# Layer 2 beyond its first 512 tokens: blocks of 256, both products by one level of Strassen's method

## The chip, the cores and the metric

One NeuronCore of a Trainium2 chip runs the whole program. The metric is device time in microseconds (us) of one execution, lower is better. TensorE multiplies matrices, VectorE (DVE in the profile) and ScalarE (ACT) do elementwise work, GpSimd (POOL) is nearly unused, and SyncE (SP) issues the DMA transfers.

## The reference

Attention with a compressive memory over 4 batches, 8 heads, 576 tokens and a head width of 64 gives an activation x of 2304 tokens by 512. Two dense layers follow, each 512 to 2048 to 512:

```python
h = x @ w_in                       # layer 1: 2304x512 by 512x2048
g = np.maximum(h, 0) + np.log1p(np.exp(-np.abs(h)))
x = g @ w_out                      # 2304x2048 by 2048x512
h = x @ w_in2                      # layer 2, the same sizes
r = np.maximum(h, 0)
return (r * r) @ w_out2
```

## The kernel before

Every 32-bit operand of a matrix product is kept as a sum of two 16-bit tensors, a high part and a low part, and each product is three matmuls (high by high, high by low, low by high) that accumulate in one PSUM bank. Attention and layer 1 (L506 to L668) are interleaved and come first. The change touches only layer 2, from L698 to L853, whose weights are W3 (512 by 2048) and W4 (2048 by 512).

Layer 2 handles the first 512 tokens plainly: `plain_h` (L715) makes the hidden activation with matmuls of 512 moving columns, in four rounds of four products of 12 matmuls, while DVE and ACT still split the pieces of W4 (`split_piece`, L404). Then `row_tile` (L817) makes the output, 128 tokens at a time: 48 matmuls whose stationary operand is a 128x128 piece of the activation and whose moving operand is 512 columns of W4.

The other 1792 tokens go in three blocks of 512 and one of 256. For them the first product is already done by one level of Strassen's method (in Winograd's form): `seven_h` (L786) makes seven products of half-size blocks in place of eight, for a pair of 128-row pieces of the hidden width at a time, four pairs to a block, 12 matmuls to a product, 336 to a block. They have 256 moving columns in the blocks of 512 tokens and 128 in the last block. The sums of weight blocks that this needs (`sums_w`, L736, into WS, four calls) and the sums of activation blocks (`x_parts`, L758, into XT) are made by DVE and ACT beside earlier matmuls. DVE adds the seven products up out of PSUM (L805 to L814), and `finish` (L708) applies the activation and splits the result into gg. The second product stays plain: `row_tile` again, 14 tiles for these tokens.

The program is written in this order, and a scheduler of the framework puts each engine's instructions in an order of its own: what comes earlier in the text goes first when it is ready, and where it isn't, later work fills in. All matmul results of this part rotate over eight PSUM banks (pool mm2, L699). Each engine works its own queue in order.

Of the kernel before, what the change touches and what calls it, by code (L numbers as in the profile page):

```python
# [17 lines left out]
P = 128  # L18
# [28 lines left out]
def kernel(  # L47
# [647 lines left out]
    w1_cm.__exit__(None, None, None)  # L695


    bp = ctx.enter_context(tc.tile_pool(name="bp", bufs=2, side="right", reuse_waits="tile"))  # L698
    mm2 = ctx.enter_context(tc.tile_pool(name="mm2", bufs=8, space=PSUM, reuse_waits="tile"))  # L699
    u2 = S_R / S_X2  # L700
    HF = NFC // 2
    gg = {}

    def new_g(j):
        gg[j] = [bp.tile([P, 2, 2, 512], F16, name=f"gg{t}_{j}", bufs=1) for t in range(2)]
        return gg[j]

    def finish(r, hi, lo):  # L708
        act.activation(r, r, AF.Relu, scale=u2)
        act.activation(r, r, AF.Square)  # L710
        act.activation(hi, r, AF.Copy)
        dve.tensor_tensor(lo, r, hi, ALU.subtract)


    def plain_h(j):  # L715
        x = x_t[0]
        new_g(j)
        for h in range(2):
            for i in range(2):
                f = h * HF + j + i  # L720
                ps = mm2.tile([P, 512], F32, tag="mm2", name="h2ps")
                for c in range(NCC):
                    wh, wl = (w[:, c, f * P:(f + 1) * P] for w in W3)
                    xh, xl = (x[:, t * NCC + c] for t in range(2))
                    pe.matmul(ps, wh, xh, start=(c == 0), stop=False)
                    pe.matmul(ps, wh, xl, start=False, stop=False)
                    pe.matmul(ps, wl, xh, start=False, stop=(c == NCC - 1))
                r = bp.tile([P, 2, 512], F32, name="r2", bufs=4)[:, 0]
                act.activation(r, ps, AF.Relu, scale=u2)
                act.activation(r, r, AF.Square)  # L730
                hi, lo = (g[:, h, :, i * 256:(i + 1) * 256] for g in gg[j])
                r = r.rearrange("p (a t) -> p a t", a=2)
                dve.tensor_copy(hi, r)
                dve.tensor_tensor(lo, r, hi, ALU.subtract)

    def sums_w(k, c0):  # L736
        c1 = slice(c0, c0 + 512)
        c2 = slice(DFF // 2 + c0, DFF // 2 + c0 + 512)
        (h11, l11), (h21, l21), (h12, l12), (h22, l22) = [
            [w[:, k + d, c] for w in W3] for d, c in ((0, c1), (0, c2), (2, c1), (2, c2))  # L740
        ]
        T = sp2.tile([P, 4, 512], F32, name="T", bufs=1)
        s1, s2, s3, s4 = (T[:, i] for i in range(4))
        dve.tensor_tensor(s1, h21, h22, ALU.add)
        dve.tensor_tensor(s3, h11, h21, ALU.subtract)
        dve.tensor_tensor(s1, s1, l21, ALU.add)
        dve.tensor_tensor(s3, s3, l21, ALU.subtract)
        dve.tensor_tensor(s1, s1, l22, ALU.add)
        dve.tensor_tensor(s3, s3, l11, ALU.add)
        dve.tensor_tensor(s2, s1, h11, ALU.subtract)  # L750
        dve.tensor_tensor(s2, s2, l11, ALU.subtract)
        dve.tensor_tensor(s4, h12, s2, ALU.subtract)
        dve.tensor_tensor(s4, s4, l12, ALU.add)
        hi, lo = (w[:, :, k, c1] for w in WS)
        act.activation(hi, T, AF.Copy)
        dve.tensor_tensor(lo, T, hi, ALU.subtract)

    def x_parts(t0):  # L758
        n = min(512, NT - t0)
        if n == 512:  # L760
            q = [[x2_at(t0 // NB + t)[:, 4 * d:4 * d + 4] for t in range(2)] for d in range(2)]
            a = 4
        else:
            q = [[x2_at(t0 // NB)[:, 4 * d + t:4 * d + 4:2] for t in range(2)] for d in range(2)]
            a = 2
        (b11, b12), (b21, b22) = q
        T = sp2.tile([P, 4, 512], F32, name="T", bufs=1)
        t1, t2, t3, t4 = (T[:, i, :n].rearrange("p (a t) -> p a t", a=a) for i in range(4))
        dve.tensor_tensor(t1, b12, b11, ALU.subtract)
        dve.tensor_tensor(t3, b22, b12, ALU.subtract)  # L770
        dve.tensor_tensor(t2, b22, t1, ALU.subtract)
        dve.tensor_tensor(t4, b21, t2, ALU.subtract)
        for i, y in enumerate((b11, b21, b22)):
            hi, lo = (z[:, i, :n].rearrange("p (a t) -> p a t", a=a) for z in XT)
# [11 lines left out]
    def seven_h(j, n):  # L786
        hn = n // 2

        def prod(w, x):
            ps = mm2.tile([P, 512], F32, tag="mm2", name="h2ps")[:, :n]  # L790
            for i in range(2):
                o = ps[:, i * hn:(i + 1) * hn]
                for k in range(2):
                    wh, wl = w3_at(w, k, j + i)
                    xh, xl = (y[:, x, k * hn:(k + 1) * hn] for y in XT)
# [3 lines left out]
            return ps  # L799

        r = [bp.tile([P, 2, 512], F32, name="r2", bufs=4) for _ in range(2)]
        (r11, r12), (r21, r22) = [[y[:, i, :n] for i in range(2)] for y in r]
        new_g(j)
        act.activation(r11, prod(0, 0), AF.Copy)
        dve.tensor_tensor(r12, prod(4, 4), r11, ALU.add)  # L805
        dve.tensor_tensor(r22, prod(5, 5), r12, ALU.add)
        dve.tensor_tensor(r21, prod(2, 6), r22, ALU.add)
        p5 = prod(3, 3)
        dve.tensor_tensor(r22, p5, r22, ALU.add)
        dve.tensor_tensor(r12, p5, r12, ALU.add)  # L810
        for h in (1, 0):
            if h == 0:
                dve.tensor_tensor(r11, prod(1, 1), r11, ALU.add)
                dve.tensor_tensor(r12, prod(6, 2), r12, ALU.add)  # L814
            finish(*(z[:, :, :n] for z in (r[h], gg[j][0][:, h], gg[j][1][:, h])))
# [67 lines left out]
```

## Time and profile before

| | us |
|---|---|
| median of 3 runs (lowest, highest) | 972.23 (971.37, 975.96) |
| the profiled execution | 977.67 |
| span of its trace, first to last instruction | 975.7 |
| TensorE busy in the span | 891.3 (91%) |
| DVE busy in the span | 657.2 (67%) |
| ACT busy in the span | 593.9 (61%) |

The trace is of one execution, 5.4 us above the median of the runs. Its span starts at 0, and the stages of layer 2 are read from about 614 us on. A busy time is the union of an engine's instructions; successive matmuls and successive DVE instructions overlap a little in the records, so the step from start to start is shorter than a duration.

### The profile page before, as it was taken

To read this page: it belongs to the slowest core of one execution; us is meant where nothing else is said; L and a number is where in the kernel's file an instruction comes from. 1 tells how busy PE (TensorE), PEld (TensorE's weight loads), DVE (VectorE), ACT (ScalarE), POOL (GpSimd) and SP (SyncE) were. 2 spreads that over 40 slices of the span, in tenths; PEclk is the share of its full clock that TensorE was granted. 3 is DMA by queue.
4 is the path that set the end of the run, shared out by engine and by line. 5 is a ranking of instruction groups with operands and counts; after the bars stand their busy time and mean duration, and the time that the engine had idled before them with its cause. 6 is when DMAs were issued, how large, how long until landed. Compare 5 with 4: busy or idle time off the path is not lost.

```text
span 975.7 us, 21743 instructions
## 1 busy us (share of the span) xinstructions
PE 891.3 (91%) x9012; PEld 682.7 (70%) x9012; DVE 657.2 (67%) x1349; ACT 593.9 (61%) x1110; POOL 2.2 (0%) x10
## 2 busy tenths in 40 slices
PE   4436899899999999999999999999999999999998
PEld 3325688788878788898887888544684585486483
DVE  7998989767747676576846499998894075066050
ACT  7865778678758786787937556562274065056051
POOL 0000000000000000000000000000000000000000
PEclk9999899899999999999999999999999999999999
DMA  9999977676669996767554475620000000000000
GB/s 233 218 244 208 230 152 162 111 116 94 108 105 168 175 152 98 109 117 131 92 87 80 60 238 173 209 65 23 22 1 12 33 1 4 29 12 1 33 13 22
DMA packets 283219, 101.05 MB, mean 104 GB/s; under 512 B 248048, under 2 KB 280816, under 8 KB 283120
## 3 DMA queue, kind: packets, MB, share of 16 engines
q1 hardware_dynamic: 282880, 99.65, 51.6%
q8 instruction: 70, 1.15, 0.5%
q14 instruction: 29, 0.24, 0.1%
q10 hardware_dynamic: 240, 0.02, 0.0%
HBM read 48.78 MB, written 4.72 MB: 55 GB/s over the span
## 4 chain that ended last, share of the span: by engine, by line
PE 56%; DMA 17%; DVE 12%; ACT 8%; issue 4%; SPq 2%; DVEq 0%; ACTq 0%
DMA PT<-p 9%; PE ops L825 6%; PE ops L824 6%; PE ops L826 6%; PE h2ps L797 4%; PE h2ps L798 4%; PE h2ps L796 4%; DMA rawv<-in_v_dram 3%; DMA rawq<-in_q_dram 3%; PE hps L431 2%; PE hps L432 2%; PE s_ps L307 2%; PE hps L433 2%; PE pvt L352 2%; DMA rawk<-in_k_dram 2%
## 5 line engine op out<-in xcount | busy, mean ns | idle before, releaser
L431 PE MATMUL hps<-x,W 128*128 128x256 f16 x576 | 158.7, 277 | 4.4 <-DVE cc L273 3.7
L432 PE MATMUL hps<-x,W 128*128 128x256 f16 x576 | 159.6, 278 | 0.1
L433 PE MATMUL hps<-x,W 128*128 128x256 f16 x576 | 159.3, 277 | 0.0
L449 PE MATMUL xps<-g,W 128*128 128x256 f16 x512 | 139.0, 273 | 1.6 <-DVE g L442 1.5
L448 PE MATMUL xps<-g,W 128*128 128x256 f16 x512 | 137.9, 274 | 2.3 <-ACT g L441 1.4
L450 PE MATMUL xps<-g,W 128*128 128x256 f16 x512 | 139.0, 273 | 0.0
L316 ACT ACTIVATE Pt<-Pt,cs 128x128 f32<-128x128 f32 (+4 forms) x144 | 84.1, 585 | 55.3 <-DVE cs L312 54.8
L307 PE MATMUL s_ps<-KT,qT 128*128 128x128 f16 (+2 forms) x992 | 83.0, 226 | 30.9 <-DVE cs L312 30.2
L825 PE MATMUL ops<-W,gg 128*128 128x512 bf16 x288 | 109.2, 379 | 0.0
L824 PE MATMUL ops<-W,gg 128*128 128x512 f16 x288 | 109.2, 379 | 0.0
L826 PE MATMUL ops<-W,gg 128*128 128x512 f16 x288 | 108.5, 379 | 0.0
L329 DVE TENSOR_TENSOR p<-Pt,p 128x512 f16<-128x512 f32 (+2 forms) x104 | 69.1, 665 | 34.3 <-ACT p L328 34.1
L307 PEld LDWEIGHTS <-qT 128*128 128x128 f16 (+1 forms) x992 | 58.6, 106 | 42.4 <-issue 37.3
L828 ACT ACTIVATE osb<-ops 128x512 f32<-128x512 f32 x18 | 10.7, 597 | 123.6 <-PE ops L826 123.6
L805 DVE TENSOR_TENSOR r<-h2ps,r 128x512 f32<-128x512 f32 (+1 forms) x16 | 9.9, 622 | 108.1 <-PE h2ps L798 107.3
L312 DVE CUSTOM_DVE_ANT_0 Pt<-s_ps,mask 128x128 f32<-128x128 f32 (+3 forms) x128 | 61.8, 483 | 27.7 <-PE s_ps L307 27.3
L352 PE MATMUL pvt<-V,PT 128*128 128x64 f16 (+1 forms) x1392 | 60.7, 198 | 18.8 <-DMA PT<-p 17.0
L352 PEld LDWEIGHTS <-PT 128*128 128x128 f16 (+1 forms) x1392 | 50.7, 104 | 28.0 <-DMA PT<-p 24.5
L328 ACT ACTIVATE p<-Pt 128x512 f16<-128x512 f32 (+2 forms) x104 | 63.0, 606 | 10.2 <-DMA PT<-p 8.9
L432 PEld LDWEIGHTS <-W 128*128 128x128 f16 x576 | 57.3, 99 | 11.8 <-issue 4.7
L798 PE MATMUL h2ps<-XT,WS 128*128 128x256 f16 (+1 forms) x256 | 63.7, 259 | 0.0
L797 PE MATMUL h2ps<-XT,WS 128*128 128x256 f16 (+1 forms) x256 | 63.7, 259 | 0.0
(157 smaller groups left out, 2072.0 us busy)
## 6 DMA issues: line engine op xcount, KB each, us to landing
wst<-in_moe_w_in_dram SPq DMA_DIRECT2D x32, 512.0 KB, 4.7
wst<-in_moe_w_out_dram SPq DMA_DIRECT2D x32, 512.0 KB, 4.5
rawk<-in_k_dram SPq DMA_DIRECT2D x16, 256.0 KB, 4.5
rawq<-in_q_dram SPq DMA_DIRECT2D x16, 256.0 KB, 4.6
rawv<-in_v_dram SPq DMA_DIRECT2D x16, 256.0 KB, 4.5
out_dram<-osb SPq DMA_DIRECT2D x16, 256.0 KB, 2.0
PT<-p SPq DMA_TRANSPOSE x100, 3.4
mraw<-in_M_prev_dram SPq DMA_DIRECT2D x8, 128.0 KB, 4.1
```

The costliest lines, as they stand in the source:

```text
L307: pe.matmul(o[x * n:(x + 1) * n], qT[g][:, t * H + h, x * n:(x + 1) * n], KT[kb][:, h, a - j * P:e - j * P], start=(t == 0), stop=(t == 1),)
L352: pe.matmul(o[r], t[:, o0 + i + y, r], V[kb][:, z, h, :], start=(i == 0 and y + z == 0), stop=(i == nb - 1 and y > 0),)
L431: pe.matmul(o, wh, x[:, c], start=(c == 0), stop=False)
L432: pe.matmul(o, wh, x[:, NCC + c], start=False, stop=False)
L433: pe.matmul(o, wl, x[:, c], start=False, stop=(c == NCC - 1))
L448: pe.matmul(ps, wh, gh, start=(f == f0), stop=False)
L449: pe.matmul(ps, wh, gl, start=False, stop=False)
L450: pe.matmul(ps, wl, gh, start=False, stop=(f == f1 - 1))
L797: pe.matmul(o, wh, xl, start=False, stop=False)
L824: pe.matmul(ps, gh, W4[0][:, f, :], start=(a == 0), stop=False)
L825: pe.matmul(ps, gh, W4[1][:, f, :], start=False, stop=False)
L826: pe.matmul(ps, gl, W4[0][:, f, :], start=False, stop=(a == NFC - 1))
```

## The change

From token 512 on, layer 2 works in seven blocks of 256 tokens (numbers 2 to 8 of nine). `seven_h` has two calls per block, each for four 128-row pieces of one half of the hidden width's halves, seven products of 24 matmuls with 128 moving columns each. The second product, too, takes Strassen's form for blocks 3 to 7: `seven_o` has seven products of 24 matmuls with 256 moving columns, four in its first call and three in its second, and adds them up in o. Blocks 2 and 8 keep a plain second product (`plain_o`, 96 matmuls of 512 columns).

New elementwise work comes with it: `sums_w4` (four calls, into WT) makes the sums of W4's blocks, and `parts` makes, for each half of a block, the sums of activation blocks (GS) beside the activation blocks themselves (GA), each split into high and low. The sums of W3's blocks (`sums`, called by `sums_w3`) take eight DVE additions in place of ten and split the result in two halves. The additions out of PSUM in `seven_h` are as many for each 512 columns as before.

Buffers are laid out anew. One tile TS of 4 x 512 per partition takes the place of T: weight sums use all of it, `x_parts` its first half and the output blocks o its second. The intermediate r of the first half-call lies in a quarter of W3 that is no longer read (RB), XT has a second copy in the room of the first 512 tokens' x, GA has three buffers and GS two. In the plain part for the first 512 tokens, r2 has three buffers of half the size in place of four, and osb one in place of three.

The order of the text per block kb is: `x_parts` of the next block, first half of `seven_h`, first call of `seven_o` for block kb-1, `parts` of the first half, second half of `seven_h`, second call of `seven_o` for kb-1, `parts` of the second half. Two calls of `sums_w4` stand after the four row tiles of the first 512 tokens, one after block 2, one inside block 3.

```diff
+NPL = 1
+W4A = (0, 2)
+W4B = {1: (4,), 2: (6,)}
...
-    bp = ctx.enter_context(tc.tile_pool(name="bp", bufs=2, side="right", reuse_waits="tile"))
+    bp_cm = tc.tile_pool(name="bp", bufs=1, side="right", reuse_waits="tile")
+    bp = bp_cm.__enter__()
...
-                r = bp.tile([P, 2, 512], F32, name="r2", bufs=4)[:, 0]
+                r = bp.tile([P, 512], F32, name="r2", bufs=3)
...
+    def sums(quarters, first, out):
+        T = TS
+        for i, (h, l) in enumerate(quarters):
+            dve.tensor_tensor(T[:, i].rearrange("p (a c) -> p a c", a=h.shape[1]), h, l, ALU.add)
+        a, b, c, d = (T[:, i] for i in range(4))
+        if first:
+            dve.tensor_tensor(d, b, d, ALU.add)
+            dve.tensor_tensor(b, a, b, ALU.subtract)
+            dve.tensor_tensor(a, d, a, ALU.subtract)
+            dve.tensor_tensor(c, c, a, ALU.subtract)
         else:
+            dve.tensor_tensor(a, b, a, ALU.subtract)
+            dve.tensor_tensor(b, d, b, ALU.subtract)
+            dve.tensor_tensor(d, d, a, ALU.subtract)
+            dve.tensor_tensor(c, c, d, ALU.subtract)
+        T = T.rearrange("p q (a c) -> p q a c", a=quarters[0][0].shape[1])
+        for i in (slice(0, 2), slice(2, 4)):
+            act.activation(out[0][:, i], T[:, i], AF.Copy)
+            dve.tensor_tensor(out[1][:, i], T[:, i], out[0][:, i], ALU.subtract)
+    def sums_w3(k, c0):
+        q = [[w[:, k + d:k + d + 1, f * DFF // 2 + c0:f * DFF // 2 + c0 + 512] for w in W3]
+             for d, f in ((0, 0), (0, 1), (2, 0), (2, 1))]
+        sums(q, True, [w[:, :, k:k + 1, c0:c0 + 512] for w in WS])
+    def sums_w4(j):
+        q = [[w[:, d * HF + j:d * HF + j + 2, m * 256:m * 256 + 256] for w in W4]
+             for d, m in ((0, 0), (0, 1), (1, 0), (1, 1))]
+        sums(q, False, [w[:, :, j:j + 2] for w in WT])
+    def x_parts(kb):
+        q = [[x2_at(kb)[:, 4 * d + t:4 * d + 4:2] for t in range(2)] for d in range(2)]
...
+        X = XT[kb % 2]
+        T = TS[:, :, :NB]
...
+    def w4_at(w, j):
+        if w < 3:
+            o, m = ((0, 0), (HF, 0), (HF, 256))[w]
+            return [y[:, o + j, m:m + 256] for y in W4]
+        return [y[:, w - 3, j] for y in WT]
+    GA, GS = {}, {}
+    def seven_h(kb, q):
+        X = XT[kb % 2]
         def prod(w, x):
+            ps = mm2.tile([P, 512], F32, tag="mm2", name="h2ps")
+            for i in range(4):
+                o = ps[:, i * P:(i + 1) * P]
                 for k in range(2):
+                    wh, wl = w3_at(w, k, 4 * q + i)
+                    xh, xl = (y[:, x, k * P:(k + 1) * P] for y in X)
                     pe.matmul(o, wh, xh, start=(k == 0), stop=False)
                     pe.matmul(o, wh, xl, start=False, stop=False)
                     pe.matmul(o, wl, xh, start=False, stop=(k == 1))
+            return ps.rearrange("p (j t) -> p j t", j=4)
+        r = RB[2 * q:2 * q + 2]
+        r11, r12, r21, r22 = r[0][:, 0], r[0][:, 1], r[1][:, 0], r[1][:, 1]
         act.activation(r11, prod(0, 0), AF.Copy)
+        dve.tensor_tensor(r12, prod(3, 4), r11, ALU.add)
+        dve.tensor_tensor(r22, prod(4, 5), r12, ALU.add)
         dve.tensor_tensor(r21, prod(2, 6), r22, ALU.add)
+        p5 = prod(6, 3)
         dve.tensor_tensor(r22, p5, r22, ALU.add)
         dve.tensor_tensor(r12, p5, r12, ALU.add)
+        act.activation(r[1], r[1], AF.Relu, scale=u2)
+        act.activation(r[1], r[1], AF.Square)
+        dve.tensor_tensor(r11, prod(1, 1), r11, ALU.add)
+        dve.tensor_tensor(r12, prod(5, 2), r12, ALU.add)
+        act.activation(r[0], r[0], AF.Relu, scale=u2)
+        act.activation(r[0], r[0], AF.Square)
+    def parts(kb, q, plain):
+        def split(dst, src):
+            act.activation(dst[:, 0], src, AF.Copy)
+            dve.tensor_tensor(dst[:, 1], src, dst[:, 0], ALU.subtract)
+        r = RB[2 * q:2 * q + 2]
+        r11, r12, r21, r22 = r[0][:, 0], r[0][:, 1], r[1][:, 0], r[1][:, 1]
+        ga = GA[kb, q] = bp.tile([P, 2, 3, 4, P], F16, name="GA", bufs=3)
+        gs = GS[kb, q] = bp.tile([P, 2, 4, 4, P], F16, name="GS", bufs=2)
+        split(ga[:, :, 1:], r[1])
+        split(ga[:, :, 0], r11)
+        if plain:
+            split(gs[:, :, 0], r12)
+            return
+        dve.tensor_tensor(r22, r12, r22, ALU.add)
+        dve.tensor_tensor(r12, r11, r12, ALU.subtract)
+        dve.tensor_tensor(r11, r22, r11, ALU.subtract)
+        dve.tensor_tensor(r21, r21, r11, ALU.subtract)
+        split(gs[:, :, :2], r[0])
+        split(gs[:, :, 2:], r[1])
+    def store(g, o):
+        for b, s0, r0, k_ in segs(g):
+            p0 = b * S + s0
+            sp.dma_start(out=out[p0:p0 + k_, :].rearrange("p (a c) -> p a c", a=2), in_=o[r0:r0 + k_])
+    OB = {}
+    PR = {1: (0, 0), 2: (1, 1), 4: (2, 5), 6: (3, 6), 7: (4, 4), 3: (5, 2), 5: (6, 3)}
+    def seven_o(kb, which):
+        def prod(n):
+            gi, wi = PR[n]
+            ps = mm2.tile([P, 512], F32, tag="mm2", name="ops")[:, :256]
+            for j in range(HF):
+                g = GA[kb, j // 4][:, :, gi] if gi < 3 else GS[kb, j // 4][:, :, gi - 3]
+                gh, gl = g[:, 0, j % 4], g[:, 1, j % 4]
+                wh, wl = w4_at(wi, j)
+                pe.matmul(ps, gh, wh, start=(j == 0), stop=False)
+                pe.matmul(ps, gh, wl, start=False, stop=False)
+                pe.matmul(ps, gl, wh, start=False, stop=(j == HF - 1))
+            return ps
+        def add(o, ps, y):
+            dve.scalar_tensor_tensor(o, ps, SO, y, ALU.mult, ALU.add)
+        if which == 0:
+            OB[kb] = TS[:, :, NB:]
+        o = OB[kb]
+        o11, o12, o21, o22 = (o[:, i] for i in range(4))
+        if which == 0:
+            act.activation(o12, prod(6), AF.Copy, scale=SO)
+            add(o21, prod(7), o12)
+            p5 = prod(5)
+            add(o22, p5, o21)
+            add(o12, p5, o12)
+            add(o12, prod(3), o12)
+            return
+        p1 = prod(1)
+        act.activation(o11, p1, AF.Copy, scale=SO)
+        add(o[:, 1:], p1.rearrange("p (a c) -> p a c", a=1).to_broadcast([P, 3, 256]), o[:, 1:])
+        add(o11, prod(2), o11)
+        store(2 * kb, o[:, :2])
+        add(o21, prod(4), o21)
+        store(2 * kb + 1, o[:, 2:])
+    def plain_o(kb):
+        o = TS[:, :, NB:].rearrange("p (t a) c -> p t a c", t=2)
+        for th in range(2):
+            ps = mm2.tile([P, 512], F32, tag="mm2", name="ops")
+            for a in range(NFC):
+                j, h = divmod(a, 2)
+                g = GS[kb, j // 4][:, :, 0] if (h, th) == (0, 1) else GA[kb, j // 4][:, :, h + th]
+                gh, gl = g[:, 0, j % 4], g[:, 1, j % 4]
+                f = h * HF + j
+                pe.matmul(ps, gh, W4[0][:, f, :], start=(a == 0), stop=False)
+                pe.matmul(ps, gh, W4[1][:, f, :], start=False, stop=False)
+                pe.matmul(ps, gl, W4[0][:, f, :], start=False, stop=(a == NFC - 1))
+            act.activation(o[:, th], ps.rearrange("p (a c) -> p a c", a=2), AF.Copy, scale=SO)
+            store(2 * kb + th, o[:, th])
...
-        o = bp.tile([P, 512], F32, name="osb", bufs=3)
+        o = bp.tile([P, 512], F32, name="osb", bufs=1)
...
+    WT = [sp2.tile([P, 4, HF, DM // 2], t, name=f"WT{i}") for i, t in enumerate((F16, BF16))]
+    TS = sp2.tile([P, 4, 512], F32, name="T")
+    XT = [[sp2.tile([P, 7, NB], F16, name=f"XT{t}") for t in range(2)]]
+    x0 = x_t[0].rearrange("p a t -> p (a t)")
+    XT.append([x0[:, i * 7 * NB:(i + 1) * 7 * NB].rearrange("p (a t) -> p a t", a=7) for i in range(2)])
+    RB = [w[:, 0:2, DFF // 2:].bitcast(F32).rearrange("p a (j t) -> p a j t", t=P) for w in W3]
+    K0 = XB // NB
+    x_parts(K0)
     for c0 in (0, 512):
         for k in range(2):
-            sums_w(k, c0)
+            sums_w3(k, c0)
+    x_parts(K0 + 1)
     for m in range(XB // P):
         row_tile(0, m, XB // 2)
-    for t0 in range(XB, NT, XB):
-        n = min(XB, NT - t0)
-        for j in range(0, HF, 2):
-            seven_h(j, n)
-        if t0 + n < NT:
-            x_parts(t0 + n)
-        for m in range(n // P):
-            row_tile(t0, m, n // 2)
+    for j in W4A:
+        sums_w4(j)
+    bp_cm.__exit__(None, None, None)
+    bp = ctx.enter_context(tc.tile_pool(name="bq", bufs=1, side="right", reuse_waits="tile"))
+    RB += [bp.tile([P, 2, 4, P], F32, name=f"r{i}") for i in range(2)]
+    def rest_w4(n):
+        for j in W4B.get(n, ()):
+            sums_w4(j)
+    for kb in range(K0, NBLK):
+        plain = kb < K0 + NPL or kb == NBLK - 1
+        if K0 < kb < NBLK - 1:
+            x_parts(kb + 1)
+        seven_h(kb, 0)
+        if K0 < kb <= K0 + NPL:
+            plain_o(kb - 1)
+        elif kb > K0:
+            seven_o(kb - 1, 0)
+        parts(kb, 0, plain)
+        rest_w4(2 * (kb - K0))
+        seven_h(kb, 1)
+        if kb > K0 + NPL:
+            seven_o(kb - 1, 1)
+        parts(kb, 1, plain)
+        rest_w4(2 * (kb - K0) + 1)
+    plain_o(NBLK - 1)
```

## Rows read from the trace of the kernel before

**Rows 1.** The page: TensorE's busy time and its 40 slices.

```profile
PE 891.3 (91%) x9012; PEld 682.7 (70%) x9012; DVE 657.2 (67%) x1349; ACT 593.9 (61%) x1110; POOL 2.2 (0%) x10
PE   4436899899999999999999999999999999999998
```

**Rows 2.** Windows by stage: length, busy us and count by engine, clock, DMA.

```profile
614.41:655.86 41.45, 41.45 (x195) 18.78 (x193) 41.38 (x81) 26.14 (x45) 0.00 (x0) 1.00 0.43 136
655.86:697.29 41.43, 41.43 (x193) 18.77 (x192) 33.72 (x46) 12.10 (x12) 0.00 (x0) 1.00 0.06 20
697.29:733.98 36.69, 36.69 (x338) 32.89 (x337) 34.87 (x50) 24.27 (x26) 0.00 (x0) 1.00 0.02 8
733.98:775.41 41.43, 41.43 (x194) 18.77 (x192) 9.81 (x11) 9.26 (x12) 0.00 (x0) 1.00 0.05 20
775.41:812.10 36.69, 36.69 (x338) 32.89 (x337) 24.77 (x34) 23.95 (x27) 0.00 (x0) 1.00 0.02 8
...
931.65:950.41 18.76, 18.76 (x337) 18.75 (x336) 13.26 (x32) 13.00 (x24) 0.00 (x0) 1.00 0.04 16
950.41:975.70 25.29, 20.89 (x99) 9.31 (x96) 2.32 (x5) 4.24 (x8) 0.00 (x0) 0.97 0.08 22
```

**Rows 3.** Waits of TensorE from 560 us on, all it lists.

```profile
PE xps L449 <- DVE g L442: 1.3, 2, 1.1
PE xps L448 <- ACT g L441: 0.3, 1, 0.3
```

**Rows 4.** Groups by shape, 931.65 to 950.41 us: busy us, mean ns, idle.

```profile
L796 PE MATMUL h2ps<-XT,WS 128*128 128x128 f16 x64 | 11.3, 219 | 0.0
...
L798 PEld LDWEIGHTS <-WS 128*128 128x128 bf16 x64 | 6.3, 98 | 0.0
```

**Rows 5.** Groups by shape of ACT from 655.86 us on.

```profile
L709 ACT ACTIVATE r<-r 128x1024 f32<-128x1024 f32 x24 | 25.2, 1051 | 33.4 <-DVE r L809 32.2 <-DVE r L814 1.1
L828 ACT ACTIVATE osb<-ops 128x512 f32<-128x512 f32 x18 | 10.7, 597 | 123.6 <-PE ops L826 123.6
L804 ACT ACTIVATE r<-h2ps 128x256 f32<-128x256 f32 x4 | 1.5, 379 | 0.0
```

**Rows 6.** Timeline of DVE, plain part's end, a weight sum (start, duration).

```profile
661.75 0.68 DVE L734 TENSOR_TENSOR gg<-r,gg 128x512 f16<-128x512 f32 x1
...
666.12 0.69 DVE L744 TENSOR_TENSOR T<-W 128x512 f32<-128x512 f16 x1
666.73 0.68 DVE L745 TENSOR_TENSOR T<-W 128x512 f32<-128x512 f16 x1
...
674.57 2.29 DVE L756 TENSOR_TENSOR WS<-T,WS 128x2048 bf16<-128x2048 f32 x1 [1.97 <-ACT WS L755]
```

**Rows 7.** Timeline of DVE, fourth weight sum beside additions from PSUM.

```profile
700.27 0.69 DVE L747 TENSOR_TENSOR T<-T,W 128x512 f32<-128x512 f32 x1
700.88 0.68 DVE L805 TENSOR_TENSOR r<-h2ps,r 128x512 f32<-128x512 f32 x1
701.48 0.68 DVE L748 TENSOR_TENSOR T<-T,W 128x512 f32<-128x512 f32 x1
702.08 0.68 DVE L749 TENSOR_TENSOR T<-T,W 128x512 f32<-128x512 f32 x1
702.68 0.68 DVE L806 TENSOR_TENSOR r<-h2ps,r 128x512 f32<-128x512 f32 x1
...
709.96 1.22 DVE L712 TENSOR_TENSOR gg<-r,gg 128x1024 f16<-128x1024 f32 x1
711.10 0.68 DVE L806 TENSOR_TENSOR r<-h2ps,r 128x512 f32<-128x512 f32 x1
```

**Rows 8.** Timeline of DVE in the last block, steps of 256 columns.

```profile
940.25 0.42 DVE L807 TENSOR_TENSOR r<-h2ps,r 128x256 f32<-128x256 f32 x1
940.59 0.41 DVE L813 TENSOR_TENSOR r<-h2ps,r 128x256 f32<-128x256 f32 x1
940.92 0.41 DVE L809 TENSOR_TENSOR r<-h2ps,r 128x256 f32<-128x256 f32 x1
```

More of the change, by code (lines that the diff above doesn't have):

```diff
@@ L695 @@
     w1_cm.__exit__(None, None, None)
-    bp = ctx.enter_context(tc.tile_pool(name="bp", bufs=2, side="right", reuse_waits="tile"))
+    bp_cm = tc.tile_pool(name="bp", bufs=1, side="right", reuse_waits="tile")
+    bp = bp_cm.__enter__()
     mm2 = ctx.enter_context(tc.tile_pool(name="mm2", bufs=8, space=PSUM, reuse_waits="tile"))
     u2 = S_R / S_X2
+    SO = 1.0 / (S_R * S_R)
     HF = NFC // 2
@@ L706, in new_g @@
         return gg[j]
[L708 to L712, printed above, removed]
     def plain_h(j):
@@ L734, in plain_h @@
                 dve.tensor_tensor(lo, r, hi, ALU.subtract)
[L736 to L762, printed above, removed]
-        else:
-            q = [[x2_at(t0 // NB)[:, 4 * d + t:4 * d + 4:2] for t in range(2)] for d in range(2)]
-            a = 2
+    def sums(quarters, first, out):
[8 more added lines that the diff above has]
+            dve.tensor_tensor(c, c, a, ALU.subtract)
+        else:
+            dve.tensor_tensor(a, b, a, ALU.subtract)
[6 more added lines that the diff above has]
+            dve.tensor_tensor(out[1][:, i], T[:, i], out[0][:, i], ALU.subtract)
@@ L766, in x_parts @@
         (b11, b12), (b21, b22) = q
-        T = sp2.tile([P, 4, 512], F32, name="T", bufs=1)
-        t1, t2, t3, t4 = (T[:, i, :n].rearrange("p (a t) -> p a t", a=a) for i in range(4))
+        X = XT[kb % 2]
+        T = TS[:, :, :NB]
+        t1, t2, t3, t4 = (T[:, i].rearrange("p (a t) -> p a t", a=2) for i in range(4))
         dve.tensor_tensor(t1, b12, b11, ALU.subtract)
@@ L773, in x_parts @@
         for i, y in enumerate((b11, b21, b22)):
-            hi, lo = (z[:, i, :n].rearrange("p (a t) -> p a t", a=a) for z in XT)
+            hi, lo = (z[:, i].rearrange("p (a t) -> p a t", a=2) for z in X)
             act.activation(hi, y, AF.Copy)
             dve.tensor_tensor(lo, y, hi, ALU.subtract)
-        act.activation(XT[0][:, 3:, :n], T[:, :, :n], AF.Copy)
-        dve.tensor_tensor(XT[1][:, 3:, :n], T[:, :, :n], XT[0][:, 3:, :n], ALU.subtract)
+        act.activation(X[0][:, 3:], T, AF.Copy)
+        dve.tensor_tensor(X[1][:, 3:], T, X[0][:, 3:], ALU.subtract)
     def w3_at(w, k, f):
@@ L784, in w3_at @@
         return [y[:, w - 3, k, f * P:(f + 1) * P] for y in WS]
-    def seven_h(j, n):
-        hn = n // 2
+    def w4_at(w, j):
[6 more added lines that the diff above has]
+        X = XT[kb % 2]
         def prod(w, x):
-            ps = mm2.tile([P, 512], F32, tag="mm2", name="h2ps")[:, :n]
-            for i in range(2):
-                o = ps[:, i * hn:(i + 1) * hn]
+            ps = mm2.tile([P, 512], F32, tag="mm2", name="h2ps")
+            for i in range(4):
+                o = ps[:, i * P:(i + 1) * P]
                 for k in range(2):
-                    wh, wl = w3_at(w, k, j + i)
-                    xh, xl = (y[:, x, k * hn:(k + 1) * hn] for y in XT)
+                    wh, wl = w3_at(w, k, 4 * q + i)
+                    xh, xl = (y[:, x, k * P:(k + 1) * P] for y in X)
                     pe.matmul(o, wh, xh, start=(k == 0), stop=False)
@@ L798, in prod @@
                     pe.matmul(o, wl, xh, start=False, stop=(k == 1))
[L799 to L803, printed above, removed]
+            return ps.rearrange("p (j t) -> p j t", j=4)
+        r = RB[2 * q:2 * q + 2]
+        r11, r12, r21, r22 = r[0][:, 0], r[0][:, 1], r[1][:, 0], r[1][:, 1]
         act.activation(r11, prod(0, 0), AF.Copy)
-        dve.tensor_tensor(r12, prod(4, 4), r11, ALU.add)
@@ L806, in seven_h @@
-        dve.tensor_tensor(r22, prod(5, 5), r12, ALU.add)
+        dve.tensor_tensor(r12, prod(3, 4), r11, ALU.add)
+        dve.tensor_tensor(r22, prod(4, 5), r12, ALU.add)
         dve.tensor_tensor(r21, prod(2, 6), r22, ALU.add)
-        p5 = prod(3, 3)
+        p5 = prod(6, 3)
         dve.tensor_tensor(r22, p5, r22, ALU.add)
         dve.tensor_tensor(r12, p5, r12, ALU.add)
[L811 to L815, printed above, removed]
+        act.activation(r[1], r[1], AF.Relu, scale=u2)
@@ L838 @@
     WS = [sp2.tile([P, 4, 2, DFF // 2], t, name=f"WS{i}") for i, t in enumerate((F16, BF16))]
-    XT = [sp2.tile([P, 7, 512], F16, name=f"XT{t}") for t in range(2)]
-    x_parts(XB)
+    WT = [sp2.tile([P, 4, HF, DM // 2], t, name=f"WT{i}") for i, t in enumerate((F16, BF16))]
[6 more added lines that the diff above has]
+    x_parts(K0)
     for c0 in (0, 512):
         for k in range(2):
-            sums_w(k, c0)
+            sums_w3(k, c0)
+    x_parts(K0 + 1)
     for m in range(XB // P):
         row_tile(0, m, XB // 2)
-    for t0 in range(XB, NT, XB):
-        n = min(XB, NT - t0)
-        for j in range(0, HF, 2):
-            seven_h(j, n)
-        if t0 + n < NT:
-            x_parts(t0 + n)
-        for m in range(n // P):
-            row_tile(t0, m, n // 2)
+    for j in W4A:
[23 more added lines that the diff above has]
+    plain_o(NBLK - 1)
 _INS = ['q', 'k', 'v', 'M_prev', 'z_prev', 'beta', 'moe_w_in', 'moe_w_out', 'moe2_w_in', 'moe2_w_out']
```

## The prediction, made before the changed kernel ran

> **What bounds the kernel now.** I began with the page's busy times and slices: TensorE is busy 91% of the span, and full in nearly every slice of layer 2, the last third [rows 1]. I then cut layer 2 into its stages [rows 2]. In each, TensorE's busy time equals the stretch's length and the granted clock is 1.00, the 2.4 GHz level; two more pairs like the stages at 733.98 and 775.41 are left out between. The view of waits shows 1.6 us of waiting in all from 560 us on, on layer 1's lines, and none in layer 2 [rows 3]. So the time after 614 us is the number of matmuls times their steps, and a saved matmul is saved time as long as DVE and ACT keep up. The steps come from lengths and counts (two or three matmuls at the edges are counted in two windows): 512 columns, 41.43 us for 192, or 215.8 ns; 256 columns, 36.69 us for 336, or 109.2 ns; 128 columns, 18.76 us for 336, or 55.8 ns [rows 2].
>
> **First product.** Before, from token 512 on, three blocks of 36.69 us and one of 18.76: 128.8 us. After, seven blocks of 2 x 7 x 24 = 336 matmuls of 128 columns, 18.76 us each: 131.3 us. That costs 2.5 us, the fixed part of a step paid on twice as many matmuls.
>
> The price hangs on the 128-column stream, which ran only in the last block. There the weight loads' busy time is the whole stretch (18.75 of 18.76 us, 336 loads of 98 ns that overlap each other), and no matmul waited [rows 2, 4]. The Trainium skill speaks against such a stream, and the trace does not agree with it: "TensorE: Matmul & The Clock Gate", section "Back-to-back issue gap", gives about 81 ns per matmul for sustained pairs of weight load and 128-column matmul. By it the 2352 matmuls would take 190.5 us and the kernel would lose some 50 us. The measured 55.8 ns, beside DVE busy 13.26 us and ACT 13.00 us of those 18.76, is what I take [rows 2].
>
> **Second product.** Before, 14 row tiles of 48 matmuls at 215.8 ns, 145.0 us. After, blocks 2 and 8 stay plain, 192 matmuls, 41.4 us; blocks 3 to 7 take 7 x 24 = 168 matmuls of 256 columns, 18.34 us each at 109.2 ns, 91.7 us. Together 133.2 us, a saving of 11.9 us. The 256-column step comes from the other product's stream; with activations as weights only 512 columns ran, and neither had a wait. With TensorE never waiting, the net is 2.5 - 11.9 = -9.4 us.
>
> **What must stay hidden: prices of DVE and ACT.** DVE steps from start to start: 512 columns 0.60 us (666.12 to 666.73, and 700.27 to 702.68), 1024 columns 1.14 us (709.96 to 711.10) [rows 6, 7], 256 columns 0.33 us [rows 8]. ACT takes 1.05 us for 1024 columns, 0.60 for 512, 0.38 for 256 [rows 5]. So `sums` is 8 x 0.60 + 2 x 1.14 = 7.1 us of DVE; `x_parts` 7 x 0.33 + 1.14 = 3.45; one half of `seven_h` 7 x 0.60 = 4.2; `parts` full 5 x 0.60 + 3 x 1.14 = 6.4, plain 2.3; both calls of `seven_o` 2.9 (six steps of 256 and one of 768, the last 0.87 by interpolation). A block in full swing costs DVE 3.45 + 8.4 + 12.8 + 2.9 = 27.6 us, and ACT about 20, beside 18.76 + 18.34 = 37.1 us of TensorE. DVE's load rises to 74%, against 24.77 + 8.43 of 78.1 us in a pair of old stages [rows 2], but it fits.
>
> **The start is tight.** While the four first row tiles run, 655.9 to 697.3, DVE has 2.1 us left from the plain part (three steps of 0.60 and one cast, the last at 661.75 [rows 6]), `x_parts` of block 2 (3.45 plus 1.05 waiting for ACT's copy) and four weight sums. In a sum before, DVE idled 1.97 us on ACT's one copy of 2048 columns [rows 6]; now the copy is halved, so each idles about 1.1: 4 x 8.25 = 33.0. That ends at 695.5, in time. Behind it stand, until the first `seven_o` can run through: `x_parts` of blocks 3 and 4 (6.9), four `sums_w4` (28.4), additions of four halves of `seven_h` (16.8), two plain `parts` (4.7), `parts` of block 3, the second but for its last split (6.4 + 5.3): 68.5 us. A backlogged DVE kept 34.87 of 36.69 us busy in the stage at 697.29 [rows 2], so I divide by 0.95: 72.1 us, done at 767.6. TensorE needs it after three halves (28.1), plain block 2 (20.7), two more halves (18.8) and 12 matmuls (1.3), at 766.2. So it waits 1.4 us. Earlier need dates (block 2's `parts` before `plain_o` at 725.4 and 730.6) are met by some 4 us. Bounds: nothing, if other work fills DVE's gaps better; 5.6 us, if all 4.2 us of block 4's first additions slip in between, as additions out of PSUM alternate with steps of a weight sum at 700.88 and 702.68 [rows 7]. I take 1.5.
>
> **In full swing** the tightest path runs through `parts` of the second half. Counted from the start of the second call of `seven_o`: its third GA buffer comes free in the middle of the last product, at 6.55; then ACT and DVE split r[1] and r11 (1.05 + 1.14 + 0.60, to 9.4), three of DVE's four sums bring r11 (to 11.2, with the fourth to 11.8), and ACT's copy and DVE's difference for the first GS split follow (1.05 + 1.14, to 13.6 with the hand-overs). The next `seven_o` needs it after 2 products (5.2 more, 7.86 in all), a half of `seven_h` (9.38) and 12 matmuls: 18.55. The slack of 5 us covers some seven foreign steps of 0.60 on DVE; I take no wait. On PSUM: a half of `seven_h` makes seven results in eight banks, so TensorE can run 9.4 us ahead of the additions.
>
> **Edits at nothing:** osb with one buffer (a row tile takes 41.43 / 4 = 10.36 us, its copy 0.60); r2 with three (DVE is 41.38 of 41.45 us busy there [rows 2], it sets the pace with either number, and TensorE has eight banks of cover; 3 us if that cover goes); the last tile's copy and store, as before; stores with two pieces per row on SP, a queue with nothing else in it by then.
>
> **The sum:** -9.4 + 1.5 = -7.9 us. Against the profiled execution's 977.67 that is 969.8; the median of the runs lies 5.4 lower, so 972.2 - 7.9 = 964.3. The kernel's runs spread by 0.5%, about what a measurement can tell from no change, 4.9 us.
>
> **Rivals.** *DVE is late at the start.* If it reaches only 87% of its time instead of 95%, the 68.5 us take 78.7 and the wait is 8.0 us; with the fillers above it reaches some 12: 971 to 975. For it: TS is one buffer for weight sums, so DVE cannot run two at once, and the chain from the page is one engine handing to another. Against: the stage at 697.29 held a weight sum and additions at once and TensorE lost nothing [rows 2, 3]. Chance 0.20.
>
> *Each block is late (slower than before).* The place is the first GS split of the second half. If every one of its steps on DVE is followed by a foreign one (six of 0.60) and the next `x_parts` (3.45) and some ACT hand-overs (1.5) go ahead of it, 13.6 becomes 22.1 against 18.55, a wait of 3.6 us in each of five blocks, 18 us: -9.4 + 18 = +8.6, about 981. It turns the sign from 1.9 us a block. For it: additions do alternate with dependent steps [rows 7]. Against: DVE is a quarter idle and TensorE may take the other half of `seven_h` first. Chance 0.13.
>
> *Weight loads stop hiding at 128 columns.* If they could not overlap, a step would be the 98 ns of a load [rows 4]: (98 - 55.8) x 2016 more such matmuls is 85 us, some 1050. The row of the last block excludes it unless DVE and ACT disturb the loads when busier than 70%. The rule of the Trainium skill named above ("TensorE: Matmul & The Clock Gate") is a milder form of this, some 50 us by itself. Chance 0.03.
>
> *The saving is not there*, because 256-column matmuls with activations as weights step slower than 109.2 ns: 120 ns would cost 840 x 11 = 9 us and leave no change. The row for 512 columns shows no such effect; it is in the second chance's 0.20.
>
> **Numbers.** Forecast 0.64, with a wait of 0 to 4.5 us: 962.8 to 967.3. Late start or dearer step 0.20, slower cases 0.16. So faster 0.64, same 0.20, slower 0.16. The range starts at 961.5 (no wait, less 1.3 for the spread of runs) and goes to 974, which takes in most of the second case.
>
> **What would show it.** Windows over the new stages: a half of `seven_h` at 9.4 us, `seven_o` at 10.5 and 7.9, granted clock 1.00; TensorE's waits in layer 2 of one to two us, in front of the first `seven_o`, released by DVE's GS splits. Wrong would be: waits on GS in every block, matmuls of 128 columns above 56 ns, or DVE's queue still holding weight sums when `seven_o` of block 3 starts.

## The result, and the profile after

The kernel before took 973.2 us (median of 4 runs, 971.37 to 975.96), the changed one 962.16 us (4 runs, 959.30 to 964.75). The ratio is 0.9883 (95% interval 0.9844 to 0.9923), 7.5 to 15.2 us faster. A second, larger comparison further down gives 0.9906 (0.9878 to 0.9933). 962.16 lies in the predicted range, 2.1 us below the predicted 964.3.

The page of the changed kernel, busy times and slices of TensorE and DVE, answers to [rows 1]:

```profile
PE 878.4 (92%) x10372; PEld 729.9 (76%) x10380; DVE 738.2 (77%) x1490; ACT 615.6 (64%) x1144; POOL 2.2 (0%) x10
PE   4436799899999899999999999999999999999998
...
DVE  7997999777747766586846589999999998867640
```

TensorE has 1360 more matmuls in the records (1368 by count; some records are missing) and less busy time, and DVE works 81 us more. How the two now run side by side is seen in the windows by stage of the changed kernel (length, busy us and count by engine, clock, DMA), against [rows 2]: the four first row tiles, the start, the four blocks in full swing, the last plain product, and then four parts of one block in full swing (half of the first product, first call of the second, the other half, second call).

```profile
648.77:690.21 41.44, 41.23 (x190) 18.78 (x193) 38.08 (x59) 13.28 (x19) 0.00 (x0) 1.00 0.06 20
690.21:785.65 95.44, 95.33 (x1272) 82.04 (x1273) 94.06 (x150) 60.48 (x75) 0.00 (x0) 1.00 0.03 10
785.65:822.75 37.10, 37.10 (x507) 35.20 (x505) 29.08 (x47) 19.61 (x26) 0.00 (x0) 1.00 0.07 20
822.75:859.85 37.10, 37.10 (x507) 35.19 (x505) 27.35 (x42) 19.11 (x25) 0.00 (x0) 1.00 0.06 19
859.85:896.95 37.10, 37.10 (x507) 35.19 (x505) 25.50 (x38) 17.35 (x21) 0.00 (x0) 1.00 0.05 16
896.95:934.05 37.10, 37.10 (x507) 35.19 (x505) 21.92 (x34) 16.50 (x21) 0.00 (x0) 1.00 0.05 16
934.05:959.50 25.45, 20.77 (x96) 9.28 (x95) 2.13 (x3) 1.66 (x3) 0.00 (x0) 1.00 0.12 32
822.75:832.13 9.38, 9.38 (x171) 9.38 (x169) 9.35 (x14) 4.29 (x6) 0.00 (x0) 1.00 0.16 44
832.13:842.61 10.48, 10.48 (x100) 9.39 (x98) 7.33 (x13) 5.96 (x8) 0.00 (x0) 1.00 0.00 0
842.61:851.99 9.38, 9.38 (x171) 9.38 (x169) 7.47 (x11) 4.28 (x7) 0.00 (x0) 1.00 0.01 3
851.99:859.85 7.86, 7.86 (x76) 7.04 (x74) 3.21 (x7) 4.58 (x7) 0.00 (x0) 1.00 0.10 32
```

A half of the first product is 168 matmuls in 9.38 us, or 55.8 ns, with DVE busy 9.35 of it; a first call of the second product is 96 in 10.48 us, or 109.2 ns. The view of waits lists nothing for TensorE in layer 2. I measure layer 2 beyond token 512 from the start of its first matmul to the start of the last: 697.29 to 970.92 before, 273.6 us; 690.21 to 954.55 after, 264.3 us. That is 9.3 us less, against the forecast of 9.4 for TensorE's steps alone. The two profiled executions differ by 16.4 us (977.67 and 961.28); the other 7.1 are the start of layer 2, at 614.41 before and 607.33 after.

What is not in the step counts is how the start came through without a wait. DVE is busy 94.06 of 95.44 us there, and TensorE does not keep the order of the text. The timeline of TensorE in the changed kernel, where block 3's second product first runs out of sums:

```profile
762.85 0.27 PE L870 MATMUL ops<-W,GS 128*128 128x256 bf16 x1
762.96 0.27 PE L871 MATMUL ops<-W,GS 128*128 128x256 f16 x1
763.07 0.22 PE L809 MATMUL h2ps<-XT,W 128*128 128x128 f16 x1
763.12 0.22 PE L810 MATMUL h2ps<-XT,W 128*128 128x128 f16 x1
...
767.20 0.22 PE L811 MATMUL h2ps<-XT,W 128*128 128x128 f16 x1
767.25 0.27 PE L869 MATMUL ops<-WT,GS 128*128 128x256 f16 x1
```

At 763.07 it leaves the second product (ops) and takes matmuls of block 4's second half (h2ps) until the first sums arrive, at 767.25, and changes over several times more: 107 of that half's 168 matmuls, 6.0 us, go ahead of the call's last ones. The scheduler had put the queue in this order; held to another, TensorE stands and waits, as an experiment below shows.

### The profile page after: what moved, and what is told of

Read it like the earlier page. It is cut to its first block, busy times and chain, and to the rows that moved or that the text cites. A ratio compares the mean times of both kernels' runs of the same rounds, so it can differ in the third digit from the quotient of the medians.

```text
span 959.5 us, 24660 instructions
## 1 busy us (share of the span) xinstructions
PE 878.4 (92%) x10372; PEld 729.9 (76%) x10380; DVE 738.2 (77%) x1490; ACT 615.6 (64%) x1144; POOL 2.2 (0%) x10
## 4 chain that ended last, share of the span: by engine, by line
PE 60%; DMA 16%; DVE 12%; ACT 6%; issue 3%; SPq 1%; DVEq 0%; ACTq 0%
DMA PT<-p 9%; PE h2ps L811 5%; PE h2ps L809 5%; PE h2ps L810 5%; PE ops L870 3%; PE ops L869 3%; PE ops L871 3%; PE hps L435 3%; PE hps L436 3%; PE hps L434 3%; PE s_ps L310 3%; DMA rawv<-in_v_dram 3%; PE pvt L355 3%; PE xps L452 2%; PE xps L453 2%
## 5 line engine op out<-in xcount | busy, mean ns | idle before, releaser
L435 PEld LDWEIGHTS <-W 128*128 128x128 f16 x576 | 57.0, 99 | 10.1 <-issue 3.4
L436 PEld LDWEIGHTS <-W 128*128 128x128 bf16 x576 | 56.9, 99 | 7.1 <-issue 0.2
L434 PEld LDWEIGHTS <-W 128*128 128x128 f16 x576 | 57.0, 99 | 6.8
L421 ACT ACTIVATE W<-wcv 128x512 f16<-128x512 f32 x64 | 40.0, 625 | 30.6 <-DVE wcv L419 30.3
L453 PEld LDWEIGHTS <-W 128*128 128x128 bf16 x512 | 50.4, 98 | 8.2 <-issue 2.5
L445 DVE TENSOR_TENSOR g<-spa,g 128x512 f16<-128x512 f32 x72 | 49.4, 686 | 9.1 <-ACT g L444 8.7
L451 PEld LDWEIGHTS <-W 128*128 128x128 f16 x512 | 50.3, 98 | 7.6 <-issue 1.7
L441 DVE SCALAR_TENSOR_TENSOR spa<-hps,spa 128x512 f32<-128x512 f32 x72 | 49.4, 686 | 8.3 <-ACT spa L440 7.9
```

The source lines that it names most:

```text
L434: pe.matmul(o, wh, x[:, c], start=(c == 0), stop=False)
L435: pe.matmul(o, wh, x[:, NCC + c], start=False, stop=False)
L436: pe.matmul(o, wl, x[:, c], start=False, stop=(c == NCC - 1))
L451: pe.matmul(ps, wh, gh, start=(f == f0), stop=False)
L453: pe.matmul(ps, wl, gh, start=False, stop=(f == f1 - 1))
```

## The experiments

Stretches are measured as above, from the first 128-column matmul to the start of the last matmul; the changed kernel's is 264.3.

**Second product plain again.** Blocks of 256 tokens stay, Strassen's form of the second product and the sums of W4 go.

```diff
-NPL = 1
-W4A = (0, 2)
-W4B = {1: (4,), 2: (6,)}
+NPL = 7
+W4A = ()
+W4B = {}
```

> Undoes half of the change: every second product is plain again (96 matmuls of 512 columns a block) and no sums of W4 are made, while the first product keeps its blocks of 256 tokens with 128-column matmuls. Theory (the time is TensorE's steps, everything else hidden): from the first matmul of the first product's blocks to the last matmul 7 x 18.76 + 7 x 20.72 = 276.4 us against 264.7 in the changed kernel, so 11.7 us slower than the changed kernel and some 2.4 slower than the kernel before (ratio to it about 1.0025). Rival (the gain came from cheaper sums of W3, other buffers or an earlier part of the program, not from the second product): within 4 us of the changed kernel, ratio to the kernel before about 0.99.

Measured: 972.42 us against 971.11 for the kernel before, ratio 1.0004 (0.9984 to 1.0025); stretch 276.1 us, 11.8 more than the changed kernel and 2.5 more than the kernel before. Its windows (first block's first product, then the whole):

```profile
688.68:707.44 18.76, 18.76 (x338) 18.76 (x337) 13.10 (x22) 10.76 (x14) 0.00 (x0) 1.00 0.04 16
688.68:965.04 276.36, 276.36 (x3025) 196.83 (x3023) 117.43 (x183) 114.18 (x147) 0.00 (x0) 1.00 0.05 15
```

In time that is between 1.6 us less and 2.4 us more than before. So the second product alone brings the gain, since all other edits are still there; the smaller blocks cost a little in the stretch, each by its count of steps. With DVE idle for more than half of the stretch, 128-column matmuls step as in the changed kernel.

**The order of the text kept.** The first matmuls of a block's second half are made to stand behind the last matmul of the second product issued before them, in TensorE's own queue:

```diff
-                    pe.matmul(o, wh, xh, start=(k == 0), stop=False)
+                    m = pe.matmul(o, wh, xh, start=(k == 0), stop=False)
+                    if after is not None and i == 0 and k == 0:
+                        tc.add_manual_dep(m.ins, after.ins.name, NO_SYNC, reason="order")
...
-        seven_h(kb, 1)
+        seven_h(kb, 1, last_o[0])
```

(NO_SYNC stands for an order without a wait, as in L497 to L501; last_o holds that last matmul.) Inside a call of the second product the scheduler stays free.

> The changed kernel with one thing added: TensorE may not start the second half of a block's first product before the first call of the second product of the block before (or the plain second product) is done, so its matmuls keep the order of the text. Theory of the prediction (DVE's backlog at the start is late by 1.4 us, bounds 0 and 5.6, even in the order of the text): waits of TensorE of 0 to 5.6 us in all, all before the second product of block 3, none later, stretch from the first 128-column matmul to the last matmul 264.7 to 270.3 us. Rival (the budget at the start was too small, and only TensorE's running ahead with the next half of 9.4 us covered it): waits of 8 to 11 us, stretch 273 to 276 us, the whole gain gone.

Measured: 968.18 us in one run, stretch 271.9, so 7.6 us are lost, between the two theories. All of it is lost in block 3's second product, 18.15 us long instead of 10.48. Its windows, with the halves before and after:

```profile
689.55:757.17 67.62, 67.62 (x937) 56.30 (x936) 66.28 (x103) 41.82 (x52) 0.00 (x0) 1.00 0.04 14
757.17:775.32 18.15, 13.57 (x100) 10.62 (x98) 18.02 (x29) 10.81 (x12) 0.00 (x0) 0.81 0.00 1
775.32:784.70 9.38, 9.38 (x171) 9.38 (x169) 5.93 (x11) 3.39 (x6) 0.00 (x0) 1.00 0.01 2
```

The timeline of TensorE in that call:

```profile
762.30 0.27 PE L879 MATMUL ops<-W,GS 128*128 128x256 f16 x1
765.86 0.28 PE L877 MATMUL ops<-WT,GS 128*128 128x256 f16 x1 [3.28 <-ACT GS L840]
...
767.77 0.40 PE L879 MATMUL ops<-WT,GS 128*128 128x256 f16 x1 [1.30 <-DVE GS L841]
767.96 0.42 PE L877 MATMUL ops<-WT,GS 128*128 128x256 f16 x1
768.17 0.42 PE L878 MATMUL ops<-WT,GS 128*128 128x256 bf16 x1
768.38 0.42 PE L879 MATMUL ops<-WT,GS 128*128 128x256 f16 x1
```

From start to start the two waits are worth 3.56 + 1.57 - 2 x 0.11 = 4.9 us, within the theory's 0 to 5.6. The rest is the clock: from 766.6 us the granted clock is at its lower level, 1.2 GHz, for 6.8 us (0.81 over the call), and some 26 matmuls step 0.213 us instead of 0.109, which costs the other 2.7. So the wait is of the size that the theory bounds, not nil; what hides it in the changed kernel is the order in TensorE's queue. DVE was not slower here: TensorE took the first sums 76.3 us after the first 128-column matmul, against 77.0 in the changed kernel. In blocks 4 to 7 nothing waits in this order either.

**One more block by Strassen's method at the start.** Block 2 as well, with the last two sums of W4 moved up:

```diff
-NPL = 1
-W4B = {1: (4,), 2: (6,)}
+NPL = 0
+W4B = {0: (4,), 1: (6,)}
```

> One more second product by Strassen's method: block 2 is no longer plain, and the last two sums of W4 move up to stand inside block 2. Theory (DVE's backlog at the start is what limits how much can be moved): TensorE's steps fall by 2.4 us, but DVE has 3.45 + 28.4 + 12.6 + 11.7 = 56.2 us of work from the end of the sums of W3, 59 us at 95 percent, while TensorE needs it after three halves (28.1) and 12 matmuls; it is 28 us late, 9.4 of that covered by running ahead, so waits of some 18 us (12 to 22) and a stretch near 280 us instead of 264.7. Rival (DVE is not the limit at the start, TensorE always finds other work): waits under 3 us, stretch 262.3 to 265.

Measured: 977.87 us in one run, stretch 279.0, where 264.3 - 2.4 = 261.9 would stand without waits: 17.1 us lost. The windows of its first 67.84 us and of the rest:

```profile
692.16:760.00 67.84, 55.91 (x809) 51.71 (x808) 66.68 (x100) 38.24 (x46) 0.00 (x0) 0.97 0.02 6
760.00:971.30 211.30, 210.23 (x2651) 188.65 (x2648) 144.22 (x226) 98.79 (x122) 0.00 (x0) 1.00 0.06 18
```

DVE is busy 98% of the first stretch while TensorE stands idle for 12 us of it. From start to start 15.4 of the 17.1 us are waits, within the theory's 12 to 22; the other 1.7 are steps at 1.2 GHz, to which the granted clock fell for 3.4 us from 725.9. More than half of what the view of waits lists stands before matmuls of the first product, released by DVE and ACT, so these too could not fill the time. DVE is the limit at the start, and the one plain block that the change leaves there is what gives DVE its time.

**The last block by Strassen's method.**

```diff
-        plain = kb < K0 + NPL or kb == NBLK - 1
+        plain = kb < K0 + NPL
...
-    plain_o(NBLK - 1)
+    seven_o(NBLK - 1, 0)
+    seven_o(NBLK - 1, 1)
```

> The last block's second product by Strassen's method too, where the kernel has it plain. TensorE's steps fall by 2.4 us. Theory (the path through the sums of the second half takes 13.6 us from the start of the second call, and nothing of a next block stands between): in the order of the text the first sums are needed at 9.2 us, a wait of 4.4 us, of which TensorE can fill up to 3.9 with the half of the other products that needs no such sums; net between -2.4 and +2.0 us, stretch 262.3 to 266.7, one wait in front of the last block's second product. Rival (the path is much longer than 13.6 because other work goes first on DVE): a wait of 8 us or more, stretch above 270.

Measured: 963.81 us in one run, stretch 262.0, no wait of TensorE in it. The full 2.4 us are gained: its queue takes the products that need no sums in between. It was then timed beside the changed kernel:

> The changed kernel once more, to compare with the kernel before and with the next one on the same chip. Theory (only layer 2 differs): its stretch from the first 128-column matmul to the last matmul is 264.5 us again, 9.3 less than before, and the ratio to the kernel before comes to 0.990 (0.988 to 0.992); the start of layer 2 moves between runs by some us in both kernels. Rival (the part before layer 2 became faster too, by the 7 us by which the two profiled runs differ): ratio 0.983.

> The last block's second product by Strassen's method too, timed. Theory: TensorE's steps fall by 2.4 us more and nothing waits, as in its first look (stretch 262.0), so 2.4 us less than the changed kernel, ratio to the kernel before 0.9875 (0.9855 to 0.9895). Rival: what it saves on TensorE it loses in the tail, in the additions and the store after the last product: no difference from the changed kernel.

Measured: the changed kernel 963.59 us (6 runs), ratio to the kernel before 0.9906 (0.9878 to 0.9933), stretch again 264.3; with the last block too 960.91 us (6 runs), ratio 0.9877 (0.9850 to 0.9905), stretch again 262.0. The windows over layer 2 beyond token 512 of the one, then of the other:

```profile
691.80:956.25 264.45, 264.45 (x3385) 232.17 (x3383) 199.84 (x308) 134.02 (x165) 0.00 (x0) 1.00 0.05 16
```

```profile
687.69:949.77 262.08, 262.08 (x3457) 239.17 (x3455) 211.41 (x324) 137.00 (x168) 0.00 (x0) 1.00 0.05 16
```

The ratio 0.9906 is 9.1 us (6.5 to 11.9), close to the stretch's 9.3, so the runs show no gain in the part before layer 2; one of up to 2.7 us would not show. The 7.1 us between the first two profiles lie in what that part varies by: layer 2 starts between 604.8 and 612.5 us over the profiles of the changed kernel and its variants, and at 614.4 in the only one of the kernel before, an execution 5.4 us above its median. The version with the last block beats the kernel before, and in TensorE's stretch the changed kernel as well, by 2.3 us in both of its profiles; the two intervals of the time overlap.

**A longer path to the sums.** In blocks 5 to 7 one DVE step on the path to the second half's sums is repeated five times:

```diff
         split(ga[:, :, 1:], r[1])
+        if q == 1 and 5 <= kb <= 7:
+            for _ in range(5):
+                dve.tensor_tensor(ga[:, 1, 1:], r[1], ga[:, 0, 1:], ALU.subtract)
```

> The changed kernel with the path through the sums of the second half made longer on purpose: in blocks 5, 6 and 7 the difference for GA of the second half is taken six times instead of once, five more DVE steps of 1.14 us, 5.7 us on the path (DVE's load in such a block goes from 27.4 to 33.1 of 37.1 us). In the changed kernel the first GS split ends 15.4 us after the start of the second call and is needed at 18.55. Theory (in full swing TensorE is covered twice, by a slack of 3.1 us and by running ahead with the next half): no wait, stretch from the first 128-column matmul to the last matmul 264.5 us as in the changed kernel, TensorE's order mixed in these blocks. Rival of the prediction (each block is late once the path is longer than its slack): 2.6 us in each of three blocks, stretch 272 us or more.

Measured: 961.00 us in one run, stretch 264.2, no wait. The window over block 5's first such call and the half that it is mixed with, 168 and 96 matmuls in 9.38 + 10.48 us:

```profile
831.85:851.71 19.86, 19.86 (x268) 18.76 (x265) 19.74 (x30) 13.42 (x17) 0.00 (x0) 1.00 0.01 2
```

The same with TensorE held to the order of the text:

> The same longer path in blocks 5 to 7, with TensorE held to the order of the text, so that only the slack is left. Theory: on top of the 271.9 us of the order of the text alone, 5.7 - 3.1 = 2.6 us in each of three blocks, about 8 us, plus up to 3 us for each time the granted clock falls after a wait: stretch 279 to 289 us. Rival (the slack is larger than the trace of the changed kernel shows, since DVE's foreign steps on the path can move behind it): under 4 us more, stretch 272 to 276.

Measured: 981.13 us in one run, stretch 282.2, 10.3 more than the order of the text alone. The three calls in question took 14.95, 14.66 and 13.02 us instead of 10.48; the windows of this kernel over them:

```profile
840.79:855.74 14.95, 12.29 (x99) 9.82 (x97) 14.43 (x20) 9.93 (x11) 0.00 (x0) 0.89 0.00 0
882.36:897.02 14.66, 12.43 (x100) 9.79 (x98) 14.13 (x19) 9.93 (x11) 0.00 (x0) 0.88 0.00 0
923.64:936.66 13.02, 10.82 (x100) 9.22 (x97) 11.00 (x16) 8.44 (x10) 0.00 (x0) 1.00 0.00 0
```

That is 11.2 us together (block 3's call was 0.9 us shorter than in the run before), 2.5 to 3.2 of waiting in each, and 1.3 each in the first two, in which the granted clock fell once more. The number agrees with the theory, its derivation doesn't. The timeline of DVE on that path, in this kernel:

```profile
833.47 1.22 DVE L850 TENSOR_TENSOR GA<-r,GA 128x1024 f16<-128x1024 f32 x1
834.60 0.69 DVE L825 TENSOR_TENSOR W<-h2ps,W 128x512 f32<-128x512 f32 x1
835.20 1.22 DVE L850 TENSOR_TENSOR GA<-r,GA 128x1024 f16<-128x1024 f32 x1
836.34 0.69 DVE L826 TENSOR_TENSOR W<-h2ps,W 128x512 f32<-128x512 f32 x1
...
838.67 1.22 DVE L850 TENSOR_TENSOR GA<-r,GA 128x1024 f16<-128x1024 f32 x1
839.80 0.69 DVE L829 TENSOR_TENSOR W<-h2ps,W 128x512 f32<-128x512 f32 x1
840.40 0.68 DVE L830 TENSOR_TENSOR W<-h2ps,W 128x512 f32<-128x512 f32 x1
841.00 0.68 DVE L833 TENSOR_TENSOR W<-h2ps,W 128x512 f32<-128x512 f32 x1
841.60 1.22 DVE L850 TENSOR_TENSOR GA<-r,GA 128x1024 f16<-128x1024 f32 x1
```

Each repeated step (L850) is followed by a foreign one (an addition out of PSUM), the fourth by three, so 5.7 us of own work made the path 10.4 us longer: ACT's copy for the first sums ends 24.0 us after the start of the second call, 13.6 without the repeats. Against that, the call has more cover than I counted: it does the halves of all four products that need only the first half's sums, 48 matmuls or 5.2 us, before it waits, not 12 matmuls. The two errors nearly cancel. Free to run ahead, TensorE hides all of it.

## Why the prediction was right, step by step

**TensorE's steps** came out to the tenth: 55.8 ns at 128 columns over all 2352 matmuls, 109.2 ns with activations as weights, first product +2.5 us (second product plain: measured 2.5 over before), second product -11.9 (11.8 between that run and the changed kernel), together -9.4 (9.3 measured).

The weight loads stayed hidden with DVE busy 9.35 of 9.38 us, so the rival on them falls. The rule of the Trainium skill that spoke for it ("TensorE: Matmul & The Clock Gate", section "Back-to-back issue gap", some 81 ns at 128 columns) does not agree with any run here, where it is 55.8. The rival of a dearer 256-column step falls by the 109.2.

**The start** was the term that was mis-sized. I put the wait at 1.5 us; the changed kernel has none, and in the order of the text it is 4.9. Two parts of the working were off. The list of DVE's work before the first sums was too short: in the run in the order of the text DVE was busy 77.3 us from 689.1 to 767.7, not 68.5:

```profile
689.10:767.71 78.61, 74.09 (x991) 61.40 (x989) 77.27 (x122) 49.74 (x61) 0.00 (x0) 0.99 0.04 12
```

Block 4's first additions (4.2), most of `x_parts` of block 5 (2.5) and some later work went in between; I had kept the additions as the upper bound only. From the end of the sums of W3 that took 78.6 us where 72.1 were forecast, 6.5 more. And the cover was 48 matmuls instead of 12, 3.9 us more. The two errors pull opposite ways, so it is partly luck that 1.5 lies so near nothing. That TensorE would run ahead stood in the prediction only under a rival, as "may take the other half", and as what the PSUM banks allow. The wait was priced without it, and it is worth the whole 7.6 us.

The rival of a late start is right that DVE comes later than forecast, though not by its reason: DVE was not at 87% of its time but busy 98%, with a longer list. Its result is wrong, because of the order in TensorE's queue. Block 2 by Strassen's method bears the size of the budget out: 56.2 us of work at 95% and 9.4 of cover gave 18 us of waits, and 15.4 came.

**Full swing**: DVE was put at 27.6 us a block, the windows show 29.08, 27.35, 25.50 and 21.92. The path was put at 13.6 us; the timeline of DVE in the changed kernel (the second call began at 814.89) gives 15.4:

```profile
822.73 1.23 DVE L833 TENSOR_TENSOR GA<-r,GA 128x1024 f16<-128x1024 f32 x1 [1.97 <-ACT GA L832]
...
827.33 0.68 DVE L818 TENSOR_TENSOR W<-h2ps,W 128x512 f32<-128x512 f32 x1
827.93 0.68 DVE L847 TENSOR_TENSOR r<-r,r 128x512 f32<-128x512 f32 x1
828.53 0.68 DVE L819 TENSOR_TENSOR W<-h2ps,W 128x512 f32<-128x512 f32 x1
829.13 1.21 DVE L833 TENSOR_TENSOR GS<-r,GS 128x1024 f16<-128x1024 f32 x1
```

The difference ends at 830.3. Foreign additions (W<-h2ps) alternate with the path's own steps, as the rival of a late block said; the slack was still there, 3.1 us by the need date of 18.55. Running ahead is not needed here: from 785.65 until the last plain product TensorE runs in the order of the text in the changed kernel, and nothing waits. In the order of the text, and with the path made longer, that rival's mechanism does show: 2.5 to 3.2 us of waiting in each block.

**The edits at nothing** cost nothing that shows: the plain part takes 41.45 us before and 41.44 after, the first row tiles 41.43 and 41.44, and from the start of the last matmul to the end it is 4.8 and 4.9. The time came out 2.1 us under the forecast. Without the wait that did not come the forecast is 962.8, and the two medians of the changed kernel, 962.16 and 963.59, lie on either side of it, so the rest is within their spread.

## What to carry to other kernels

Where TensorE is full and its waits are none, a change to the algorithm can be priced by counting matmuls and reading the step of each width from a stretch that runs it, provided the work that it hands to other engines is added up stage by stage with dates; the sum over the kernel says nothing about the stage that is full. In that sum a chain of dependent steps on a busy shared engine should be counted with a foreign step behind each (here seven behind five), and the cover must include what the scheduler can move ahead in the waiting engine's queue: taken away, it turned 9.3 us of gain in the stretch into 1.7.

## What the runs showed of the hardware that I had not expected

A short wait can cost more than its length. In the order of the text TensorE waited 3.4 us in block 3's call, ran four matmuls and waited again; during that second wait, of 1.5 us, the granted clock fell to 1.2 GHz, stayed there for 6.8 us and cost a further 2.7 us. In the longer path in the order of the text it fell after waits of 1.6 and 0.8 us in block 5's call and at the end of two such waits in block 6's, each time for 3.4 us at a cost of 1.3; after waits of 1.6 and 0.9 us in block 7's it did not fall. So the lengths of these waits alone do not say when it falls.

A stream of 128-column matmuls ran for 9.38 us at a time with the weight loads' busy time equal to the whole stretch, as in the last block before, and here with DVE busy 9.35 of it: it lost nothing.
